# mLSTM and feed-forward on one core: other start addresses for the activation tiles and three of the output-weight tiles

## Chip, core and metric

One core of a Trainium2 chip runs the whole program. The metric is the device time of one execution in microseconds (us). The kernel before takes 466.67 us, the median of three runs (466.32 to 467.1).

## What is computed

A gated linear-attention recurrence (mLSTM) over 4 batches x 8 heads x 768 tokens with a head width of 40, and behind it a feed-forward of 3072 tokens x 320 channels through 2048 hidden channels:

```python
m_new  = max(f[t] + m, i[t])
f_stab = exp(f[t] + m - m_new);  i_stab = exp(i[t] - m_new)
C = f_stab * C + i_stab * outer(v[t], k[t])
n = f_stab * n + i_stab * k[t]
y[t] = sigmoid(o[t]) * (C @ q[t]) / max(abs(n . q[t]), 1)
...
h = x @ w_in                       # x: y of all heads side by side, 3072 x 320
out = (max(h, 0) + alpha * min(h, 0)) @ w_out
```

## The kernel before

The recurrence is computed in chunks of 128 tokens, two chunks make a group of 256 tokens, and there are twelve groups. Each group's attention result is transposed, so that channels lie on partitions, and split into a high and a low part (`x_tiles_of`, `split_steps`): XH and XL hold channels 0 to 255 (two slices of 256 tokens), X2 and X2L the last 64 channels. All matmuls of the feed-forward work on such float32r pairs.

**Up** (`FeedForward.up_steps`, lines 713 to 720). A step makes two of the 16 blocks of 128 hidden channels: for each, eight matmuls accumulate in PSUM. The stationary operand is a 128x128 piece of a weight tile (WH, WL or W2), the moving one a slice of 256 tokens of XH, XL, X2 or X2L. Eight steps a group and twelve groups make 96 steps, so 1536 matmuls of 256 columns.

**Down** (`FeedForward.down`, line 750). The hidden activations, again as a high part gh and a low part gl, are the stationary operand (128x128 pieces). The moving operand is a 320-column row of the output weights, of the high tile OH or the low tile OL. There are four OH tiles and four OL tiles (OH0 to OH3, OL0 to OL3), each with four rows. A step issues eight matmuls that alternate between OH and OL, each such pair with the same piece of gh, and then four of gl with OH. This makes 12 matmuls a step and, with 96 steps, 1152 in all.

```python
def high(e, j):
    add(e, j, gh, OH, start=fp + e == 0, stop=False)
    add(e, j, gh, OL, start=False, stop=False)
def low(e, j):
    add(e, j, gl, OH, start=False, stop=2 * fp + e == NF - 1)
```

In group 1 the first four steps keep gh and gl in one tile gg (tags sp0 and sp1) rather than in the tiles of the late pool.

**Order.** The order of all work is a list of step names (`ORDER` and `PATTERN`), and `pin` ties each engine to it. TensorE runs the steps of the feed-forward between the chunks' small matmuls; ScalarE, VectorE and GpSimd make g, gh and gl from the PSUM tile ph, and the SyncE queue issues the DMAs.

**Places.** A tile's start within a partition comes from the order in which the pools hand out room: the pool `const` holds the weights and the constants, behind it lie the pool `sb` (attention tiles, X's tiles) and the pool `late` (g, gh, gl, ob). While weights are loaded as 64-bit words, the places of OH1, OL1 and so on serve as staging tiles first (`staging`, with the table `ROOM`), so `staging` is what claims the place of OL1, OL2 and OL3. `LPs` holds two tiles of 512 bytes a partition for a three-part copy of the decay rows; the steps lqa to lqe that would fill the first of them (LP0) are defined but stand in no order list.

Of the kernel before, what the change touches and what calls it, by code (L numbers as in the profile page):

```python
# [8 lines left out]
F32 = mybir.dt.float32  # L9
F32R = mybir.dt.float32r  # L10
U32 = mybir.dt.uint32
BF16 = mybir.dt.bfloat16
# [5 lines left out]
def kernel(ctx: ExitStack, tc: tile.TileContext, q, k, v, i_gate, f_gate, o_gate, w_in, w_out, alpha, out):  # L18
# [3 lines left out]
    P = 128  # L22
    BH = B * H
# [3 lines left out]
    GT = GC * P  # L27
# [6 lines left out]
    const = ctx.enter_context(tc.tile_pool(name="const", bufs=1))  # L34
# [30 lines left out]
    def out_block(i):  # L65
        OH[i] = const.tile([P, NB, DM], F32R, tag=f"OH{i}", name=f"OH{i}")
        OL[i] = const.tile([P, NB, DM], F32R, tag=f"OL{i}", name=f"OL{i}")

    def staging(name, tag):
        t = const.tile([P, NB * DM], U32, tag=tag, name=name)  # L70
        return t[:, : 2 * CW].rearrange("p (c w) -> p c w", w=2)

# [10 lines left out]
    C_t = [const.tile([P, H, VA], F32, tag=f"C{i}", name=f"C{i}") for i in range(3)]  # L83
    L_d = dram.tile([NC, BH, P], F32, tag="L_d", name="L_d")

    LPs = [const.tile([3 * BH, GT], BF16, tag=f"LP{k}", name=f"LP{k}") for k in range(2)]
    unit = const.tile([BH, 1], F32, tag="unit", name="unit")
    gam = const.tile([BH, NC], F32, tag="gam", name="gam")
    const.tile([P, 64], F32, tag="room", name="room")
# [761 lines left out]
    def load_w_in(i, kt):  # L851

        c0 = i * CW
        half, h0 = divmod(c0, DH)

        def part(X):

            def at():
                if X[half] is None:
                    in_half(half)  # L860
                return X[half][:, kt, h0 : h0 + CW]

            return at

        src = w_in[kt * P : (kt + 1) * P, c0 : c0 + CW]
        return Weights(f"wi{i}_{kt}", staging(f"wi{i}_{kt}", ROOM[i][kt]), [(slice(0, P), src, part(WH), part(WL))])

    def load_w_rest(i):

        pieces = []  # L870
        for e in range(2):
            cs = slice((i + e) * CW, (i + e + 1) * CW)
            rows, other = (slice(x * KR, (x + 1) * KR) for x in (e, 1 - e))
            pieces.append((rows, w_in[2 * P :, cs], W2[rows, cs], W2[other, cs]))
        return Weights(f"wr{i}", staging(f"wr{i}", ROOM[i][2]), pieces)
# [44 lines left out]
    def first_group():  # L920
# [14 lines left out]
        f, i, rst, m = fi[:, 0, :S], fi[:, 1, :S], rm[:, 0, :S], rm[:, 1, : S + 1]  # L935
# [171 lines left out]
        def one(it):  # L1107
            return lambda: next(it)
# [3 lines left out]
        def add(names, it):  # L1112
            for name in names.split():
                steps[name] = one(it)
# [14 lines left out]
        def lazily(make):  # L1129

            def run():
                yield from make()
            return run()

        def alpha_by_token():
            pa = psa("pa")
            nc.tensor.transpose(pa[:, :NF], al, ident[:NF, :NF])
            yield
            nc.vector.tensor_scalar(oma, pa[:, :NF], -1.0, 1.0, ALU.mult, ALU.add)
            yield  # L1140
# [25 lines left out]
        def decay_parts(k, tag):  # L1166

            rest = late_pool.tile([P, 512], F32, tag=tag, name=f"L_rest{k}", bufs=3)[:BH]
            rest, mid = rest[:, :GT], rest[:, GT:].bitcast(BF16)[:, :GT]
            Lt, LP = L[:, k * GT : (k + 1) * GT], LPs[k]  # L1170
            nc.scalar.copy(LP[:BH], Lt)
            yield
            nc.gpsimd.tensor_tensor(rest, Lt, LP[:BH], ALU.subtract)
            yield
            nc.scalar.copy(mid, rest)
            yield
            nc.scalar.copy(LP[BH : 2 * BH], rest)
            yield
            nc.gpsimd.tensor_tensor(LP[2 * BH :], rest, mid, ALU.subtract)
            yield  # L1180
# [59 lines left out]
            do2=lambda: load_gate(0, nc.sync, 2 * GC, NC), do3=lambda: load_gate(1, nc.sync),  # L1240
        )
        add("lpa lpb lpc lpd lpe", lazily(lambda: decay_parts(1, "gl")))
        add("lqa lqb lqc lqd lqe", lazily(lambda: decay_parts(0, "gh")))
        add("alT alC", alpha_by_token())
        add("bTt bTc", by_token(bj, bT, "b", 0, 0, GC))
        add("wTt wTc", by_token(wj, wT, "w", 0, 0, GC))
# [61 lines left out]
    start = len(nc.cur_bb.bb.instructions)  # L1308
    ffs = {}
    first = first_group()  # L1310
    next(first)
    pin(start)
# [30 lines left out]
```

## Time and profile before

| | |
|---|---|
| median of three runs | 466.67 us (466.32 to 467.1) |
| the profiled execution's own time | 465.87 us |
| its span, first to last instruction | 464.2 us |
| TensorE busy | 458.3 us, 99% of the span |
| weight loads busy | 447.5 us |
| VectorE, ScalarE, GpSimd busy | 308.7, 313.8, 309.1 us |
| DMA engines, mean busy share | 58.1% by the main queue |
| granted TensorE clock | 1.000 |

TensorE's matmul time and its weight loads are two rows that overlap: a matmul's record reaches from the start of its stream to its last result, so records of neighbours overlap too, and what a matmul costs is read from the distance between two starts.

### The profile page before, as it was taken

How to read it: one execution, taken by the hardware profiler on the slowest of the kernel's cores; microseconds unless marked ns; L12 is line 12 of the kernel's file. 1: busy time of each engine (PE TensorE's matmuls, PEld its weight loads, DVE VectorE, ACT ScalarE, POOL GpSimd, SP SyncE). 2: the span in 40 equal slices, each digit the busy share in tenths (PEclk: the TensorE clock that was granted, in tenths of full speed). 3: DMA queues.
4: the chain of work that ended last, by engine and by line, in shares of the span. 5: the costliest groups of instructions: out<-in, count | busy, mean ns of one | idle time of the engine just before them, and what ended most of it. 6: DMA issues, size and time to landing. Idle time of an engine off the chain costs nothing.

```text
span 464.2 us, 11823 instructions
## 1 busy us (share of the span) xinstructions
PE 458.3 (99%) x4434; PEld 447.5 (96%) x4434; DVE 308.7 (67%) x659; ACT 313.8 (68%) x714; POOL 309.1 (67%) x398
## 2 busy tenths in 40 slices
PE   8999999999999999999999999999999999999997
PEld 6889999999999999999999999999999999999996
DVE  4798999576866766766666775775675675663321
ACT  4799998858857857758758758658758658423331
POOL 7635656746879579479779589479789587224241
PEclk9999999999999999999999999999999999999999
DMA  8998897759694573696783683598572341000000
GB/s 187 215 269 196 221 254 213 141 133 186 150 144 113 138 160 96 133 184 160 137 169 91 125 181 97 117 186 172 128 165 84 96 136 42 1 28 1 30 2 28
DMA packets 156163, 61.61 MB, mean 133 GB/s; under 512 B 140154, under 2 KB 145834, under 8 KB 156106
## 3 DMA queue, kind: packets, MB, share of 16 engines
q1 hardware_dynamic: 156026, 60.75, 58.1%
q8 instruction: 35, 0.57, 0.5%
q14 instruction: 22, 0.18, 0.1%
q10 hardware_dynamic: 80, 0.11, 0.1%
HBM read 36.90 MB, written 4.03 MB: 88 GB/s over the span
## 4 chain that ended last, share of the span: by engine, by line
PE 90%; DVE 4%; ACT 2%; SPq 2%; DMA 1%; issue 1%; DVEq 0%; ACTq 0%
PE po L750 36%; PE ph L713 5%; PE ph L718 5%; PE ph L716 5%; PE ph L714 5%; PE ph L717 5%; PE ph L720 5%; PE ph L715 5%; PE ph L719 5%; PE pH L376 4%; PE pS L477 4%; PE pH L337 1%; PE p L566 1%; PE pu L181 1%; PE pI L401 1%; PE pS L1071 1%
## 5 line engine op out<-in xcount | busy, mean ns | idle before, releaser
L739 POOL TENSOR_TENSOR gl<-g,gh 128x512 fp32r<-128x512 f32 x74 | 95.9, 1297 | 37.6 <-ACT gh L737 30.8
L750 PE MATMUL po<-OH,gh 128*128 128x320 f32 x368 | 110.4, 311 | 0.0
L750 PE MATMUL po<-OL,gh 128*128 128x320 f32 x368 | 109.3, 309 | 0.0
L723 ACT ACTIVATE g<-ph 128x512 f32<-128x512 f32 x96 | 57.4, 598 | 72.1 <-PE ph L720 66.5
L728 DVE SCALAR_TENSOR_TENSOR g<-g,oma,ph 128x256 f32<-128x256 f32 x148 | 63.5, 471 | 37.3 <-ACT g L723 37.3
L750 PEld LDWEIGHTS po<-OL,gh 128*128 128x128 f32 x368 | 69.2, 188 | 0.0
L750 PEld LDWEIGHTS po<-OH,gh 128*128 128x128 f32 x368 | 69.1, 188 | 0.0
L750 PE MATMUL po<-OH,gl 128*128 128x320 f32 x368 | 69.1, 309 | 0.0
L713 PE MATMUL ph<-XH,WH 128*128 128x256 f32 x192 | 57.6, 300 | 0.5 <-DVE g L728 0.5
L750 PEld LDWEIGHTS po<-OH,gl 128*128 128x128 f32 x368 | 57.7, 188 | 0.3 <-DVE gl L739 0.3
L718 PE MATMUL ph<-XL,WH 128*128 128x256 f32 x192 | 53.7, 280 | 0.0
L714 PE MATMUL ph<-XH,WH 128*128 128x256 f32 x192 | 53.6, 279 | 0.0
L716 PE MATMUL ph<-XH,WL 128*128 128x256 f32 x192 | 53.6, 279 | 0.0
L717 PE MATMUL ph<-X,W 128*128 128x256 f32 x192 | 53.6, 279 | 0.0
L719 PE MATMUL ph<-XL,WH 128*128 128x256 f32 x192 | 53.6, 279 | 0.0
L715 PE MATMUL ph<-XH,WL 128*128 128x256 f32 x192 | 53.6, 279 | 0.0
L720 PE MATMUL ph<-X2L,W 128*128 128x256 f32 x192 | 53.6, 279 | 0.0
L363 ACT CAST E<-pS 128x512 bf16<-128x512 f32 x72 | 41.1, 581 | 15.2 <-DVE pS L360 14.6
L448 ACT ACTIVATE E<-Lb,gates 128x128 f32<-128x128 f32 x160 | 50.1, 393 | 0.0
L737 ACT CAST gh<-g 128x512 fp32r<-128x512 f32 x74 | 44.7, 617 | 7.4 <-DVE g L728 4.9
L360 DVE TENSOR_TENSOR pS<-pS,E 128x512 f32<-128x512 f32 x36 | 24.9, 696 | 31.3 <-PE pS L477 23.5
L451 POOL TENSOR_SCALAR_AFFINE_SELECT E<-E 128x512 f32<-128x512 f32 x40 | 26.7, 668 | 20.4 <-ACT E L448 20.3
(196 smaller groups left out, 1136.8 us busy)
## 6 DMA issues: line engine op xcount, KB each, us to landing
Lb<-L_d SPq DMA_DIRECT2D x20, 512.0 KB
wo<-in_moe_w_out_dram SPq DMA_DIRECT2D x8, 640.0 KB
wi<-in_moe_w_in_dram SPq DMA_DIRECT2D x8, 512.0 KB
qn<-in_q_dram SPq DMA_DIRECT2D x24, 160.0 KB
kn<-in_k_dram SPq DMA_DIRECT2D x24, 160.0 KB
og<-in_o_gate_dram SPq DMA_DIRECT2D x24, 160.0 KB
va<-in_v_dram SPq DMA_DIRECT2D x24, 160.0 KB
out_dram<-ob SPq DMA_DIRECT2D x11, 320.0 KB
```

Of the source, the lines that this page charges most:

```text
L713: nc.tensor.matmul(dst, WH[half][:, 0, hs], XH[:, 0], start=True, stop=False)
L714: nc.tensor.matmul(dst, WH[half][:, 1, hs], XH[:, 1], start=False, stop=False)
L715: nc.tensor.matmul(dst, WL[half][:, 0, hs], XH[:, 0], start=False, stop=False)
L716: nc.tensor.matmul(dst, WL[half][:, 1, hs], XH[:, 1], start=False, stop=False)
L717: nc.tensor.matmul(dst, W2[:, fs], X2, start=False, stop=False)
L718: nc.tensor.matmul(dst, WH[half][:, 0, hs], XL[:, 0], start=False, stop=False)
L719: nc.tensor.matmul(dst, WH[half][:, 1, hs], XL[:, 1], start=False, stop=False)
L720: nc.tensor.matmul(dst, W2[:, fs], X2L, start=False, stop=True)
L723: nc.scalar.activation(gt, ph, AF.Relu, scale=-1.0)
L728: nc.vector.scalar_tensor_tensor(out=y[:, e], in0=gt[:, e], scalar=oma[:, f : f + 1], in1=ph[:, e], op0=ALU.mult, op1=ALU.add)
L739: (nc.vector if split else nc.gpsimd).tensor_tensor(gl, y, gh.bitcast(F32), ALU.subtract)
L750: nc.tensor.matmul(po[j], x[:, e, j * P : (j + 1) * P], W[f // NB][:, f % NB], **ends)
```

## The change

Three edits in the set-up code; all 8136 instructions of the built program, their order and their waits are the same in both kernels, and only the addresses differ.

```diff
+    GAP = {"OL1": 16, "OL3": 48, "OL2": 32}
+
     def staging(name, tag):
+        if tag in GAP:
+            const.tile([P, GAP.pop(tag)], F32, tag=f"gap{tag}", name=f"gap{tag}")
         t = const.tile([P, NB * DM], U32, tag=tag, name=name)
...
-    LPs = [const.tile([3 * BH, GT], BF16, tag=f"LP{k}", name=f"LP{k}") for k in range(2)]
+    LPs = [None, const.tile([3 * BH, GT], BF16, tag="LP1", name="LP1")]
...
-        add("lqa lqb lqc lqd lqe", lazily(lambda: decay_parts(0, "gh")))
```

Unused tiles of 64, 192 and 128 bytes are put ahead of OL1, OL3 and OL2, in the order in which those are claimed, and LP0 (512 bytes) goes. The places that the pools give, in bytes of a partition:

| tiles | start before | modulo 256 | start now | modulo 256 |
|---|---|---|---|---|
| W2 | 17408 | 0 | 17408 | 0 |
| WH1, WL1, WH0, WL0 | 47616 to 72704 | 0 | 512 less | 0 |
| OH0, OL0 | 80896, 86016 | 0, 0 | 512 less | 0, 0 |
| OH1, OL1 | 91136, 101376 | 0, 0 | 90624, 100928 | 0, 64 |
| OH2, OL2 | 96256, 116736 | 0, 0 | 95744, 116608 | 0, 128 |
| OH3, OL3 | 106496, 111616 | 0, 0 | 106048, 111360 | 64, 0 |
| Lb, kS, Z (gg), E, og, kd, qS | 121856 to 174080 | 0 | 128 less | 128 |
| XH, XL, X2, X2L | 188224 to 199488 | 64 | 128 less | 192 |
| gl, g, gh, ob | 208192 to 226624 | 64 | 128 less | 192 |

The tiles ahead of LP0 (qn, kn, va, gates, C and the smaller constants) stay where they were. The two va tiles start at 33792 and 36480, which is 0 and 128 modulo 256, and the second chunk in each lies 1344 bytes further on, at 64 and 192.

## Rows read from the trace of the kernel before

**Rows 1.** The page: busy time, TensorE's clock in 40 slices, chain by engine.

```profile
PE 458.3 (99%) x4434; PEld 447.5 (96%) x4434; DVE 308.7 (67%) x659; ACT 313.8 (68%) x714; POOL 309.1 (67%) x398
...
PEclk9999999999999999999999999999999999999999
...
PE 90%; DVE 4%; ACT 2%; SPq 2%; DMA 1%; issue 1%; DVEq 0%; ACTq 0%
```

**Rows 2.** The page's groups, down and up matmuls: out<-in, count, busy us, mean ns.

```profile
L750 PE MATMUL po<-OH,gh 128*128 128x320 f32 x368 | 110.4, 311 | 0.0
L750 PE MATMUL po<-OL,gh 128*128 128x320 f32 x368 | 109.3, 309 | 0.0
...
L750 PE MATMUL po<-OH,gl 128*128 128x320 f32 x368 | 69.1, 309 | 0.0
L713 PE MATMUL ph<-XH,WH 128*128 128x256 f32 x192 | 57.6, 300 | 0.5 <-DVE g L728 0.5
...
L714 PE MATMUL ph<-XH,WH 128*128 128x256 f32 x192 | 53.6, 279 | 0.0
```

**Rows 3.** Waits of TensorE: total us, times, longest us.

```profile
PE warm L154 <- POOL ident masks.py:199: 1.4, 1, 1.4
PE ph L713 <- DVE g L728: 0.5, 1, 0.5
PE pg L1161 <- DVE gates L979: 0.4, 1, 0.4
PE pb L1030 <- DVE E L1075: 0.3, 1, 0.3
```

**Rows 4.** The chain from 443 us on: start us, length us, what; repeats merged.

```profile
443.06 0.11 PE ph L714
...
444.88 0.11 PE ph L714
...
446.46 0.12 PE ph L720
446.58 1.76 PE po L750 x12
448.33 0.12 PE ph L713
...
450.22 0.12 PE ph L713
...
452.10 8.81 PE po L750 x60
```

**Rows 5.** All matmul records of line 714: duration ns min/median/max.

```profile
L714 PE MATMUL ph<-XH,WH x192: 276/280/283, 34.8 to 451.1; 128*128 128x256 f32 x192
```

**Rows 6.** The whole chain: a bfloat16 stretch of 256 columns, and a down stretch.

```profile
28.08 0.44 PE warm L154 x4
...
81.74 3.52 PE po L750 x24
```

**Rows 7.** Instructions that touch the tile gg: duration ns, first and last start.

```profile
L750 PE MATMUL po<-OH,gg x32: 308/309/389, 76.1 to 88.5; 128*128 128x320 f32 x32
```

**Rows 8.** GpSimd and ScalarE reading the two va tiles: duration ns min/median/max.

```profile
L349 POOL TENSOR_TENSOR vr<-va,vb x18: 819/828/1287, 78.2 to 380.6; 128x336 f32<-128x336 f32 x18
...
L347 ACT CAST vb<-va x18: 462/472/475, 77.5 to 374.4; 128x336 bf16<-128x336 f32 x18
```

**Rows 9.** Two stretches: busy us of each engine, clock, DMA share, GB/s.

```profile
0.00:60.00 60.00, 57.93 (x528) 51.81 (x529) 46.92 (x97) 48.93 (x111) 34.78 (x58) 1.00 0.91 221
60.00:464.20 404.20, 400.41 (x3908) 395.69 (x3906) 261.80 (x563) 264.89 (x605) 274.35 (x340) 1.00 0.54 120
```

## The prediction

> **What bounds the kernel now.** I read the page first. TensorE's matmul row is busy for 458.3 of 464.2 us, its clock is fully granted in all 40 slices, and the chain that ended last lies on TensorE for 90% [rows 1]. It waits for others hardly at all: its four waits sum to 2.6 us [rows 3]. So the time is the sum of the distances between matmul starts, and nearly all of it lies in two kinds of matmul, those of the up step (256 columns) and of the down step (320 columns) [rows 2].
>
> Records of neighbours overlap, so I take distances from starts in the chain. The last group shows both kinds with little else running [rows 4]. In the first up stretch, L714 at 443.06 and L714 sixteen matmuls on at 444.88 are 1.82 us apart: **113.8 ns** each. In the next one, L713 at 448.33 and L713 sixteen on at 450.22 are 1.89 us apart: **118.1 ns** each. The down stretch takes 8.81 us for 60, **146.8 ns** each. All of it runs at the full clock [rows 1].
>
> The reader should see two things here. First, both are longer than the columns need: four bfloat16 matmuls of 256 columns in a row take 0.44 us, 110 ns each [rows 6]. By that, 320 columns would take 137.5 ns. The surplus is 8.1 ns on an ordinary up matmul and 9.3 ns on a down matmul. Second, the same up step on the same tiles exists in two states, 4.35 ns apart. Which is common can be read from the length of the records of L714: shortest 276, median 280, longest 283 ns [rows 5], and their mean is 279 [rows 2]. If 276 is the short state and 280 the ordinary one, at most a quarter are short. I take 1,400 of 1,536 up matmuls as ordinary.
>
> **The change part by part.** It adds, removes and moves no instruction. No wait is added and no queue changes, so each edit can act only through what one instruction takes at its new addresses.
>
> *LP0 and the steps lqa to lqe go.* No instruction ever used them: 0 us.
>
> *VectorE, ScalarE and GpSimd at other addresses.* GpSimd reads the va tiles at all four places modulo 256 that occur here (0, 64, 128 and 192) in 819 ns at the least and 828 ns in the median; ScalarE does in 462 to 475 ns [rows 8]. An effect of the place is under 3% of such an instruction. These engines are busy for 65 to 68% of the time outside the first 60 us [rows 9], and TensorE waits for VectorE 0.5 us once in that path [rows 3]. 0 us, and 3% more on each would still be hidden.
>
> *DMAs to and from other places.* Most staging tiles and the attention tiles now start off the 256-byte mark. In the first 60 us the DMA engines are busy for 0.91 of the time, after that for 0.54 [rows 9]. Transfers that take a tenth longer would still fit into the idle 5.4 us of the first stretch, DMA has 1% of the chain [rows 1], and TensorE waits for none [rows 3]: 0 us. Without that cover, a tenth of 60 us would be late at most.
>
> *Stationary gh at 192 instead of 64, against OH at 0.* The tile gg gives this for another place: it starts at 0 modulo 256, and all down matmuls between 76.1 and 88.5 us use it [rows 7]. The stretch of 24 at 81.74 lies inside and takes 3.52 us, 146.7 ns each [rows 6], against 146.8 with gh at 64 [rows 4]. Moving the stationary operand 64 bytes against the moving one did nothing. I take 0 for this edit. No row has a difference of 128 or 192. The bounds are therefore the whole surplus as a gain, 1,152 x 9.3 ns = 10.7 us, and as a loss the largest step between two states that the rows hold, the 4.35 ns of the up step: 1,152 x 4.35 ns = 5.0 us. I keep to 0, since the one shift that the trace holds gave 0.
>
> *OL1, OL2, OL3 and OH3 off the 256-byte mark.* Before, each stream of a down step starts at the place where the one before it ended, because 1,280 bytes are five times 256. Now the pairs OH1-OL1, OH2-OL2 and OH3-OL3 jump by 64, 128 and 192 bytes there and back. A jump occurs in the trace only where an up stretch (X at 64) meets a down stretch (OH at 0). There the last up matmul to the first down matmul is at 446.46 to 446.58, 0.12 us by the rounding of the chain, so a jump costs or saves less than what a row shows. I take 0, with the same bounds as above for three quarters of the down matmuls.
>
> *X's tiles at 192 instead of 64, against W at 0.* This is the term that I expect to move. The two states of the up step show that 4.35 ns hang on how its two operand streams meet, since the tiles, the clock and the shapes are the same in both. The start of the moving stream against the weights is what the change shifts, by half of the 256 bytes. If every ordinary stretch went to the short state, that would be 1,400 x 4.35 ns = 6.1 us; if none did, 0; if all went as far the other way, 6.1 us more. Both states recur in the trace with one and the same pair of addresses, so the place does not fix the state alone. I take half of the stretches: 700 x 4.35 ns = **3.0 us gained**. TensorE ahead by 3 us in 464 asks 0.7% more of the other engines, which their idle third covers.
>
> The profiled execution would go from 465.87 us (span 464.2 and 1.7 around it) to 462.9. It lies 0.8 below the median of 466.67, so the median goes to **463.7 us**.
>
> At one place a rule speaks against any effect at all. The Trainium skill, "TensorE: Matmul & The Clock Gate", section "Step-by-step: what each phase is for", says that TensorE has two independent read ports, one for the streaming operand and one for the weight load, so that loading the next weights takes nothing from the running matmul. By that rule no place could matter and the sum would be 0. The equal down stretches [rows 4, 6] agree with it; the two states of the up stretch [rows 4] do not obviously, since something other than columns and clock sets them.
>
> **The rivals.**
>
> *No effect.* The surplus is a fixed cost of 4-byte operands, and the state of an up stretch comes from when it starts and not from where its tiles lie. For it: gg against gh, and two states with the same addresses [rows 4, 6, 7]. Against it: sums of over 2,600 matmuls have to agree to 0.35 ns each to stay within 0.93 us. Time 466.7. Chance 0.25.
>
> *The short state is lost, or a third, longer one appears.* Place: the up stretches and the down matmuls with OL1 to OL3, where streams now start away from where the last one ended. Price: as far above the ordinary distance as the short one is below, 4.35 ns. It decides from 214 matmuls on (0.93 us), 14 of the 96 up steps or a fifth of the down ones. For half of the up matmuls and none of the down ones it gives 3.0 us, 469.7 us; for all up ones 472.8. For it: before the change the stationary operand of the down step starts 64 bytes behind the moving one modulo 256 (gh at 64, OH at 0), and that step carries the larger surplus; after it the up step has this difference (W at 0, X at 192). Against it: the short state is rare already, so little can be lost there. Chance 0.30.
>
> That the change does not do what it says is excluded: the addresses are those of the built program.
>
> **How the numbers follow.** Faster by the up stretches, or by the down ones, has chance 0.45 and, at half of the ordinary up stretches, 463.7 us. About 0.2%, 0.93 us, is what a measurement of this kernel can tell from no change; the first rival has all of the middle, 0.25, and the second is all of the slower side, 0.30. The range: its low end is all up stretches short (6.1 us) and a third of the down bound (3.5 us), 457 us; its high end takes the second rival to nearly all up stretches, 472 us. The likeliest case alone reaches from 457 to 465.7.
>
> **What would show it.** Right: two L714 starts sixteen matmuls apart in the middle groups stand 1.82 us apart and not 1.89, and the median record of L714 falls from 280 towards 276 ns, while a down stretch stays near 146.7 ns a matmul. Down stretches that take less than 146 ns or more than 148 ns on OL1, OL2 or OL3 but not on OL0 would show that I sized the jumps wrong at 0. DMAs are the cause if starts at 60 us are later and the distances are the same. The forecast is wrong if the up stretches keep 118.1 ns everywhere, and its sign is wrong if they take 120 ns or more.

## The result and the profile after

The changed kernel takes **462.08 us** (median of four runs, 461.66 to 462.53) against 466.5 us of the kernel before beside it (465.71 to 467.1): ratio 0.9907, 95% interval 0.9888 to 0.9925. That is 4.4 us less by the medians. The profiled execution has an own time of 461.96 us and a span of 460.2 us, 4.0 us less than the 464.2 of before.

The page after, to be laid beside [rows 1]: busy time, TensorE's clock, the chain by engine.

```profile
PE 454.4 (99%) x4434; PEld 443.7 (96%) x4434; DVE 310.1 (67%) x659; ACT 314.0 (68%) x714; POOL 308.5 (67%) x398
...
PEclk9999999999999999999999999999999999999999
...
PE 90%; DVE 4%; ACT 2%; SPq 2%; DMA 1%; issue 1%; DVEq 0%; ACTq 0%
```

TensorE's busy time fell by 3.9 us, nearly all of the span's 4.0; no other engine moved by more than 1.4 us, the clock is full in all 40 slices in both, and the chain has the same shares. So the time went out of the matmuls themselves, at the same clock. The groups of matmuls and TensorE's waits after, to be laid beside [rows 2] and [rows 3]:

```profile
L754 PE MATMUL po<-OH,gh 128*128 128x320 f32 x368 | 109.8, 311 | 0.0
L754 PE MATMUL po<-OL,gh 128*128 128x320 f32 x368 | 108.9, 307 | 0.0
...
L717 PE MATMUL ph<-XH,WH 128*128 128x256 f32 x192 | 57.5, 299 | 0.4 <-DVE g L732 0.4
```

```profile
PE warm L158 <- POOL ident masks.py:199: 1.4, 1, 1.4
PE ph L717 <- DVE g L732: 0.4, 1, 0.4
PE pg L1165 <- DVE gates L983: 0.3, 1, 0.3
PE pb L1034 <- DVE E L1079: 0.3, 1, 0.3
```

The groups' means hardly move, since records overlap. The distances show it. The chain over the last two up stretches after, for [rows 4]: start us, length us, what.

```profile
439.15 0.12 PE ph L717
...
441.10 0.11 PE ph L718
...
442.80 1.74 PE po L754 x12
444.54 0.12 PE ph L717
...
446.38 0.11 PE ph L717
...
448.20 8.79 PE po L754 x60
```

Each up stretch here has 32 matmuls. The last one lasts from 444.54 to 448.20: 3.66 us, 114.4 ns each, where before it lasted from 448.33 to 452.10: 3.77 us, 117.8 ns each [rows 4]. Within it the first sixteen take 1.84 us (115 ns each) and the second sixteen 1.82 us (113.8 ns each): the stretch begins long and goes over to the short state. The down stretch of 60 takes 8.79 us against 8.81 [rows 4]. The records of one line, for [rows 5]:

```profile
L718 PE MATMUL ph<-XH,WH x192: 276/277/287, 34.8 to 447.2; 128*128 128x256 f32 x192
```

The median fell from 280 to 277 with the shortest still 276: the short state was there before, and now most matmuls are in it. The two stretches of the span, for [rows 9]:

```profile
0.00:60.00 60.00, 57.95 (x531) 51.91 (x531) 47.41 (x97) 49.10 (x111) 34.20 (x58) 1.00 0.91 221
60.00:460.20 400.20, 396.46 (x3907) 391.77 (x3904) 262.64 (x563) 264.95 (x604) 274.30 (x340) 1.00 0.55 121
```

By 60 us TensorE has run 531 matmuls against 528 before, with the same DMA share of 0.91, so the transfers to the new places do not show as a delay. The 4.0 us come from the 400 us behind.

To see the whole, I summed the distance from each matmul record's start to the next one's over the trace of each run, apart for the 1,536 up matmuls, the down matmuls and the rest (small matmuls and every wait between). From before to after the up sum goes from 184.53 to 181.14 us (3.39 less), the down sum from 170.11 to 169.63 (0.48 less), the rest from 104.53 to 104.45. Those add to 3.94 us, the 4.0 of the span. Up matmuls at 115 ns or less (the short state, mean 113.4 ns) went from 175 to 1,012, those between 115 and 125 ns from 1,312 (mean 117.8 ns) to 474 (mean 118.5). Some 50 are left in each; 43 of these are the first matmul of a stretch, which takes some 200 ns both before and after. Of the 79 unbroken up stretches, 5 before and 66 after are short: their mean distance from the ninth matmul on is at most 115 ns. The table of the experiments holds these sums for all runs.

### The profile page after: what moved, and what is told of

Its sections match the earlier page's. It is cut to its first block, busy times and chain, and to the rows that moved or that the text cites. A ratio compares the mean times of both kernels' runs of the same rounds, so it can differ in the third digit from the quotient of the medians.

```text
span 460.2 us, 11823 instructions
## 1 busy us (share of the span) xinstructions
PE 454.4 (99%) x4434; PEld 443.7 (96%) x4434; DVE 310.1 (67%) x659; ACT 314.0 (68%) x714; POOL 308.5 (67%) x398
## 4 chain that ended last, share of the span: by engine, by line
PE 90%; DVE 4%; ACT 2%; SPq 2%; DMA 1%; issue 1%; DVEq 0%; ACTq 0%
PE po L754 36%; PE ph L717 5%; PE ph L720 5%; PE ph L718 5%; PE ph L719 5%; PE ph L722 5%; PE ph L721 5%; PE ph L724 5%; PE ph L723 5%; PE pH L380 4%; PE pS L481 4%; PE pH L341 2%; PE p L570 1%; PE pu L185 1%; PE pI L405 1%; PE pS L1075 1%
```

## The experiments

The theory to be tested: what counts is where X's tiles start against the weights modulo 256 bytes, and the other edits do little. Against it: the gain comes from the jumps of the OL tiles, from gh and the other late tiles, from LP0, or from the absolute place of X. The sums of all runs:

| run | up us | down us | rest us | matmuls up to 115 ns | short stretches of 79 | median us, ratio to before [95%] |
|---|---|---|---|---|---|---|
| before | 184.53 | 170.11 | 104.53 | 175 | 5 | 466.5 |
| after | 181.14 | 169.63 | 104.45 | 1,012 | 66 | 462.08, 0.9907 [0.9888, 0.9925] |
| e1_x_alone | 181.53 | 169.91 | 104.72 | 874 | 49 | 462.94, 0.9930 [0.9914, 0.9947] |
| e2_ol_alone | 184.17 | 169.71 | 105.35 | 265 | 12 | 465.38, 0.9981 [0.9967, 0.9994] |
| e3_lp0_out | 184.85 | 170.10 | 104.98 | 112 | 4 | 466.57, 1.0013 [1.0002, 1.0023] |
| e4_late_alone | 185.13 | 170.03 | 105.50 | 17 | 1 | 466.23, 1.0005 [0.9994, 1.0017] |
| e5_w_moved | 180.90 | 170.30 | 105.29 | 1,051 | 60 | 462.9, 0.9920 [0.9905, 0.9935] |
| e6_x_at_0 | 187.79 | 170.16 | 106.33 | 9 | 0 | 468.99, 1.0061 [1.0038, 1.0084] |
| e7_x_at_128 | 186.46 | 169.92 | 104.95 | 292 | 0 | 467.7, 1.0024 [1.0013, 1.0035] |
| e8_all_64 | 181.27 | 169.24 | 105.55 | 959 | 64 | 462.01, 0.9899 [0.9882, 0.9915] |
| e9_x_at_224 | 185.94 | 170.15 | 105.50 | 69 | 0 | 467.42, 1.0021 [1.0011, 1.0031] |
| e10_x_at_160 | 185.56 | 169.98 | 105.15 | 171 | 0 | 467.19, 1.0014 [1.0000, 1.0027] |
| e11_ol_192 | 180.73 | 169.68 | 105.01 | 1,088 | 69 | 462.46, 0.9910 [0.9894, 0.9925] |
| e12_x_at_96 | 188.16 | 170.07 | 105.34 | 67 | 0 | 469.27, 1.0065 [1.0053, 1.0078] |

The rest varies between 104.5 and 106.3 us from profile to profile (in e6, which has the most, the granted clock was 0.86 between 12 and 24 us, before the first up matmul), so a difference of under 1 us is read from the up and down sums and from the times together, not from one span.

### One part at a time

**X alone at 192** (e1). LP0 is out as in the change; padding keeps everything but X's tiles where it was modulo 256.

```diff
     def x_tiles_of(g):
+        if g == 0:
+            sb.tile([P, 32], F32, tag="xpad", name="xpad", bufs=1)
...
     late_pool = ctx.enter_context(tc.tile_pool(name="late", bufs=2))
+    late_pool.tile([P, 32], F32, tag="lpad", name="lpad", bufs=1)
```

> LP0 is out, and of all tiles only X's start at another place modulo 256: 192 instead of 64. gh, gl, the attention tiles and the OL tiles keep their places modulo 256 (everything behind LP0 lies 512 bytes lower). Theory X (the place of X against the weights sets the state of the up stretches): up stretches lock at 113.3 ns a matmul as in the changed kernel, the sum of the up distances falls from 184.5 to about 181.1 us, the time by 3 to 4 us to about 463. Theory OL (the jumps of the down step hand the up stretches another start, and that sets their state): no change, 466.5 us, up at 117.8 ns. Theory late (the place of gh and the other late tiles): no change, 466.5 us.

Measured: 462.94 us against 466.24 beside it, 3.3 us less, with the up sum 3.0 us down. The last up stretch and the records of the line:

```profile
445.48 0.12 PE ph L715
...
449.11 8.80 PE po L752 x60
```

```profile
L716 PE MATMUL ph<-XH,WH x192: 276/278/282, 35.1 to 448.1; 128*128 128x256 f32 x192
```

3.63 us for 32 matmuls, 113.4 ns each. By the medians X alone brings three quarters of the change's 4.4 us; the intervals of the two ratios overlap.

**The jumps of OL1 to OL3 alone** (e2), with LP0 out and X back at 64.

```diff
+    GAP = {'OL1': 16, 'OL3': 48, 'OL2': 32}
...
+        if tag in GAP:
+            const.tile([P, GAP.pop(tag)], F32, tag=f"gap{tag}", name=f"gap{tag}")
...
+    sb.tile([P, 32], F32, tag="spad", name="spad", bufs=1)
```

> The gaps ahead of OL1, OL2 and OL3 as in the change, and all tiles behind them back at their old places modulo 512 (X and gh at 64). Theory X: up stretches stay at 117.8 ns, only the down step moves, by half a microsecond or less: 466 us. Theory OL: up stretches lock at 113.3 ns, about 463 us. Theory late: 466 us.

Measured: ratio 0.9981, about 0.9 us less. The chain over the last up stretch and the down stretch behind it:

```profile
448.44 0.12 PE ph L718
...
452.21 8.78 PE po L755 x60
```

The up stretch keeps its 3.77 us; the down stretch of 60 takes 8.78 us against 8.81. The down sum fell by 0.40 us, more than it differs between the other runs with X at 64 and no jumps (170.03 to 170.30). The up sum fell by 0.36 us, less than it differs between before, e3 and e4 (184.53 to 185.13), which have X at this place too. In this one profile the rest is 0.8 us longer and the span is the 464.2 us of before, so the 0.9 us stand on the ten executions and not on the profile. The jumps are not quite free of effect, then: they give a little in the down matmuls.

**LP0 out alone** (e3) and **the late pool alone at 192** (e4, gh, gl, g and ob, with X at 64). e3 has only the change's two lines on LP0; e4 has these and the line of the late pool from e1.

> Only LP0 and its unused steps are out: every tile behind it lies 512 bytes lower, W2 and the tiles ahead of it do not move. All three theories (X, OL, late): 466.5 us, no change, up at 117.8 ns and down at 146.7 ns. If it is faster by 3 us, the 512 bytes between W2 and the other weights, or the bits above 256, are the cause, and none of the three.

> LP0 is out, and the late pool alone (t, g, gl, gh, ob) starts at 192 instead of 64 modulo 256; X stays at 64, OL at 0. Theory X: up stretches stay at 117.8 ns, 466.5 us; the down step has its stationary operand moved by 128 against OH, which I forecast at 0. Theory late: up stretches lock at 113.3 ns or the down step falls below 146 ns a matmul, 463 us. Theory OL: no change.

Measured: 1.0013 and 1.0005, down sums 170.10 and 170.03 against 170.11. Both stay within 0.2% of before. The end of the chain in e4:

```profile
453.60 8.81 PE po L750 x60
```

The down stretch of 60 takes the 8.81 us of [rows 4], though gh now stands at 192 against OH at 0: moving the stationary operand of the down step did not move its time at this difference either, as gg had shown at another. The runs with X at 64 also say how firm the ordinary state is there: 112 short matmuls in e3, 17 in e4 and 265 in e2, against 175 before.

### The place of X against the place of W

**W moved instead of X** (e5): all up weights go to 128 modulo 256, X stays at 64, so the difference X minus W is 192 again, with neither at the place that it has in the change.

```diff
+    const.tile([P, 32], F32, tag="wpad0", name="wpad0")
     W2 = const.tile([P, DFF], F32R, tag="W2", name="W2")
+    const.tile([P, 32], F32, tag="wpad1", name="wpad1")
...
+        const.tile([P, 32], F32, tag="wpad2", name="wpad2")
         fi, rm = (const.tile([P, 2, DH], F32, tag=t, name=f"g_{t}") for t in ("WH1", "WL1"))
...
         in_half(0)
+        const.tile([P, 32], F32, tag="wpad3", name="wpad3")
         out_block(0)
```

> LP0 is out; all weights of the up step (W2, WH, WL) start at 128 instead of 0 modulo 256, and X stays at 64: the difference of X minus W modulo 256 is 192, as with X alone moved, but reached from the other side. All other tiles keep their places modulo 256. Theory relative (only the difference between X and the weights counts): up stretches lock at 113.3 ns, up sum about 181.5 us, time 463. Theory absolute (the place of the moving stream alone counts, or of X's writers): up stays at 117.8 ns, 184.8 us, time 466.5.

Measured: 0.9920, up sum 180.90, 60 short stretches. The last one:

```profile
445.79 0.12 PE ph L715
...
449.43 8.81 PE po L752 x60
```

3.64 us for 32, as in e1. It is the difference of the two operands' starts that counts, not the place of X by itself. The places also bear out the modulus for this difference: it is 192 modulo 512 in the change, 448 modulo 512 in e1, e8 and e11, and the short state is common in all four.

**X at 0, 128, 224, 160 and 96** (e6, e7, e9, e10, e12): e1 with other sizes of the two pads, so that only X's place differs from e3. The cut shows what e6 changes in e1.

```diff
-            sb.tile([P, 32], F32, tag="xpad", name="xpad", bufs=1)
+            sb.tile([P, 48], F32, tag="xpad", name="xpad", bufs=1)
...
-    late_pool.tile([P, 32], F32, tag="lpad", name="lpad", bufs=1)
+    late_pool.tile([P, 16], F32, tag="lpad", name="lpad", bufs=1)
```

> LP0 is out; X alone starts at 0 modulo 256 (difference to W: 0), everything else as with X alone at 192. Theory four places (the start of X against W in steps of 64 sets the state): some value of its own, between 113.3 and 120 ns on the up step, up sum between 180.5 and 187 us. Theory two places (192 is good, all others are alike): up at 117.8 ns, 184.8 us, 466.5.

> LP0 is out; X alone starts at 128 modulo 256 (difference to W: 128). Theory four places: a value of its own between 113.3 and 120 ns, up sum between 180.5 and 187 us. Theory two places: up at 117.8 ns, 184.8 us, 466.5.

> LP0 is out; X alone starts at 224 modulo 256, 32 bytes beyond 192, W at 0. Theory steps of 64 (what counts is which 64-byte piece of 256 both streams stand in): as X alone at 192, up sum about 181.5 us, time 463. Theory sliding (the distance itself counts, and 192 lies on a slope that leads to 0, where 120 ns was measured): up sum between 181.5 and 187.8 us, about 184.5, time 466.

> LP0 is out; X alone starts at 160 modulo 256, halfway between 128 (up sum 186.5 us) and 192 (181.5 us). Theory steps of 64: 160 stands in the same piece as 128, up sum about 186.5 us, time 467.7. Theory sliding: up sum about 184 us, time 465.5, or below 181.5 if the best place lies between.

> The kernel before without LP0, with X's tiles at 96 modulo 256 (W at 0, everything else as before modulo 256). So far only a difference of 192 gave many up matmuls of 113.3 ns; 0, 128, 160 and 224 gave 118 to 120 ns. 'One place': 192 stands alone, so 96 gives an up sum of 184.5 to 187 us, fewer than 300 matmuls of at most 115 ns, and 466.4 to 468 us. 'A second place': the good places recur within the 256 bytes (192 is good and 96 is half of it), so 96 gives an up sum near 181.5 us, over 800 such matmuls and 462.9 us.

Measured: all five are slower than before or at its edge, by 0.14% to 0.65%; e3, their control with X at 64, is 0.13% slower, so e7, e9 and e10 stand out from it by their up sums (185.56 to 186.46 against 184.85 us) and not by their times. The last up stretch of 32 in e6, e12 and e10, each with the first down row behind it:

```profile
453.38 0.12 PE ph L715
...
457.21 8.81 PE po L752 x60
```

```profile
452.68 0.12 PE ph L715
...
456.52 8.81 PE po L752 x60
```

```profile
449.87 0.12 PE ph L715
...
453.63 8.81 PE po L752 x60
```

At a difference of 0 the stretch takes 3.83 us, 119.7 ns each; at 96 3.84 us, 120.0 ns; at 160 3.76 us, 117.5 ns. In the other two it takes 3.80 us at 128 (118.8 ns) and 3.79 at 224 (118.4 ns). The down stretch of 60 is the same 8.81 us in all three rows, so the down step did not move. The median over the 79 stretches of their mean distances (from the ninth matmul on) is 120.0 at 0, 117.8 at 64, 120.0 at 96, 118.6 at 128, 117.6 at 160, **113.4 at 192**, 118.6 at 224. Thus there are more kinds of state than two. At 0 nearly every distance is 120 ns; the matmul records of e6, shown here, have a median of 283 ns where the ordinary state has 280, and the weight loads beside them, the first row, one of 192 ns where that line has 188 both before and after. At 96, 128, 160 and 224 a stretch has no steady distance: the last one of e12 repeats 117, 125, 116, 123, 119 and 120 ns. So the values of these four places are averages, and the 292 matmuls up to 115 ns of e7 are single ones within longer stretches.

```profile
L716 PEld LDWEIGHTS ph<-XH,WH x192: 187/192/192, 36.6 to 456.1; 128*128 128x128 f32 x192
L716 PE MATMUL ph<-XH,WH x192: 278/283/296, 36.7 to 456.2; 128*128 128x256 f32 x192
```

The place is neither a slope (160 and 224, the neighbours of 192 at 32 bytes, have no short stretch at all) nor a pattern that repeats within 256 (96 is on average as slow as 0, where I had allowed up to 187 us for its up sum and it took 188.16). 192 stands alone among the seven places that were run. 32 was not run. All tiles of this program start at multiples of 32 bytes, so padding reaches no place between.

### The down step's pairs

**All four pairs 64 apart** (e8): the change, with each OL at 64 and each OH at 0. **OL at 192** (e11): the change, with OL1 to OL3 at 192, all else of the output weights at 0.

```diff
-    GAP = {"OL1": 16, "OL3": 48, "OL2": 32}
+    GAP = {'OH1': 48, 'OL1': 16, 'OH3': 48, 'OL3': 16}
...
+        if i == 0:
+            const.tile([P, 16], F32, tag="gapOL0", name="gapOL0")
```

```diff
-    GAP = {"OL1": 16, "OL3": 48, "OL2": 32}
+    GAP = {'OL1': 48, 'OH3': 16, 'OL3': 48}
```

In both, one more pad in the pool `sb` keeps the tiles behind at their places of the change modulo 256. The question is whether the distance within a pair sets the time of the down step, or something else.

> X, the attention tiles and the late tiles as in the change (192, 128, 192); all four OH tiles at 0 modulo 256 and all four OL tiles at 64. In the changed kernel the matmuls with OH1 and OL1 (0 and 64) took 437.2 ns for three against 440 ns before, those with OH2 and OL2 (0 and 128) 440.1. Theory pairs (the distance of OL from OH sets the down step, and 64 is worth 2.7 ns in three): the down sum falls by another 0.5 us to about 169.1 us, time about 461.5. Theory phase (what the down step gains depends on the order of states and not on the pair): down within 0.3 us of the changed kernel, 462.

> X, the attention tiles and the late tiles as in the change; OH tiles and OL0 at 0 modulo 256, OL1, OL2 and OL3 at 192. Theory pairs (the distance of OL from OH sets the down step): in the changed kernel OL3, 192 beyond its OH3, took 143.9 ns; with three such pairs the down sum falls by about 0.5 us against the changed kernel, to 169.1 us, time 461.5. Theory phase (the order of states decides): down within 0.3 us of the changed kernel's 169.6 us, time 462.

Measured: e8 462.01 us, e11 462.46 us, neither distinguishable from the 462.08 of the change. The end of the chain in e8, and in e11:

```profile
445.27 0.13 PE ph L720
...
449.05 8.77 PE po L757 x60
```

```profile
444.70 0.12 PE ph L718
...
448.35 8.82 PE po L755 x60
```

The down stretch of 60 holds steps of the pairs 1 to 3 (OH1 with OL1 and so on). It takes 8.77 us with the pairs 64 apart and 8.82 with them 192 apart. The down sums are 169.24 and 169.68: e8 came out near the 169.1 that the theory of pairs asked for, e11 at the 169.6 of the change that the theory of phase asked for.

The single tiles say more. In the change, where each pair has another distance, the mean distance from a matmul on OH or OL to the next one (without the few over 160 ns) was 146.1 and 147.1 ns in pair 0 (apart by 0), 144.9 and 146.6 in pair 1 (by 64), 148.0 and 144.6 in pair 2 (by 128), 146.8 and 143.9 in pair 3 (OH at 64, OL at 0), against 146.6 to 147.0 for all eight before. So a jump shifts time between the two matmuls of a pair and saves at most some 3 ns on one of them. In e11 the three pairs that are 192 apart differ among themselves: one matmul on OH, one on OL and one of gl together take 437.1 ns in pair 1 and 436.6 in pair 3, where OH has the saving (144.1 and 144.0 ns), but 441.3 in pair 2, where OL takes 149.2; before they took 439.9, 439.5 and 440.4. The distance within the pair modulo 256 alone does not set it, therefore. Modulo 512 pairs 1 and 3 of e11 are 192 apart and pair 2 is 448 apart; whether that is the reason, no run shows.

The e8 rows also hold a counter-example to a simple rule. X is at 192 there, and still the last up stretch takes 3.78 us for 32, 118.1 ns a matmul, and never reaches the short state. 15 of the 79 stretches of e8 stay out of the short state, and 13 of those of the change.

## Why the prediction was right

The forecast was 463.7 us, faster by the up stretches; measured were 462.08 us. For the profiled execution it was 462.9 against 461.96; of these 0.9 us, 0.4 are X's term, 0.5 the down step and 0.1 the rest. By its own steps:

- **What bounds the kernel.** Right. TensorE's busy time and the span fell by nearly the same amount (3.9 and 4.0 us), and no other engine followed or hindered it.
- **X at 192: half of 1,400 ordinary matmuls times 4.35 ns, 3.0 us.** Right in kind: one part alone (e1) does it, it depends on the difference between the operands' starts (e5), and it works by moving stretches into the short state that the trace before already held. The term was undersized: 3.4 us in the change's up sum. The price of a matmul was near (117.8 less 113.4 is 4.4 ns, 4.35 forecast). The share was not: I took half of the stretches, and 61 more of 79 went over. Against that stand fewer ordinary matmuls to begin with, 1,312 and not 1,400, and the stretches' first matmuls. 837 more short matmuls at 4.4 ns would be 3.7 us; 3.4 was left, since the 474 that stayed out take 118.5 ns on average and not 117.8 (0.3 us). Part of these stand at the start of a stretch, which begins long. The timeline of TensorE in the changed kernel shows such a beginning (start us, length us, engine, line, what):

```profile
439.10 0.28 PE L718 MATMUL ph<-XH,WH 128*128 128x256 f32 x1
...
439.58 0.28 PE L722 MATMUL ph<-XL,WH 128*128 128x256 f32 x1
439.69 0.28 PE L723 MATMUL ph<-XL,WH 128*128 128x256 f32 x1
...
440.03 0.28 PE L718 MATMUL ph<-XH,WH 128*128 128x256 f32 x1
440.14 0.28 PE L719 MATMUL ph<-XH,WL 128*128 128x256 f32 x1
```

From 439.10 to 439.58 it is four distances of 120 ns each; from 439.69 to 440.14 four of 112.5, both within the rounding of the rows. This stretch goes over after some six matmuls. In most stretches of the change four or five distances are long first, in most of e1 and e5 two.
- **Why half.** The reason given, that the place does not fix the state alone, holds: in e8 one stretch with X at 192 is ordinary throughout. But "shifted by half of the 256 bytes" was not what made the difference: moving X by that half from 0 to 128 gains 1.3 us in the up sum and leads to no short stretch. The trace before had rows of one difference alone, 64, so it could show that a short state exists, not at which difference it is common. The sign was therefore a choice between two sides, as the chance of 0.45 said, and that it came out faster was luck: of the six other places that were run against 64, only 192 is faster.
- **gh at 192: 0.** Right, by e4 (170.03 against 170.11 us).
- **LP0, the other engines, the DMAs: 0 each.** Right for LP0, by e3 (within 0.2%). For the others the rows after agree: TensorE's waits sum to 2.4 us against 2.6, and the two stretches show no delay. The attention tiles at 128 were not run alone.
- **The jumps of OL1 to OL3: 0.** Mis-sized, slightly. The change's down sum fell by 0.48 us and e2's by 0.40 (e1's, without any jump, by 0.20); e2's time says 0.9 us, with an interval from 0.3 to 1.5. The sign that the prediction named for this came: under 146 ns on OL2 and OL3 (144.6 and 143.9), not on OL0 (147.1). The argument for 0, one jump at the seam of two stretches that cost less than a row shows, could not see 3 ns on a matmul of 147.
- **Rival "No effect".** Fallen, since e1 and e5 exclude it. The rule of the Trainium skill that was held against the change ("TensorE: Matmul & The Clock Gate", section "Step-by-step: what each phase is for", two independent read ports) gave 0 for every place as the prediction read it, and the runs do not agree with that reading: 113.4 against 120.0 ns at the full clock, for one and the same instructions, by the place alone. Whether the weight load takes anything from the running matmul is a narrower question that these runs do not answer. The down step's indifference to gh agrees with the rule.
- **Rival "the short state is lost, or a third, longer one appears".** The third state exists, and at half its price: 120.0 ns, 2.2 above the ordinary one where 4.35 were assumed. It belongs to the difference 0 and, as an average, to 96, not to 192. The evidence that it gave, the down step's surplus at "stationary 64 behind moving", was no guide to the up step. Had X been moved by 64 the other way, to 0, this rival would have been the outcome: e6, 468.99 us.

What sets these states is not shown by any run. That the weight load's stream and the moving stream of the matmul beside it meet in some way that depends on their starts modulo 256 is an argument from the trace (both run at the same time, 443.7 and 454.4 us of 460.2, and in e6 the weight load's records lengthen too, from 188 to 192 ns), and no experiment here took the one away from the other. Why X alone leaves 30 stretches out of the short state, e5 19, and the change, e8 and e11 only 10 to 15, is open too. Each count is from one execution, and the medians of e1 and e5 (462.94 and 462.9 us) do not differ. The late tiles with X at 192 and everything else as before were not tried.

## What to carry to other kernels

Where TensorE bounds a kernel, measure the distance between starts of equal matmuls in several stretches: two values at one clock and one shape are a reason to try whether the operands' placement has a price, which here was up to 6.6 ns of 120 on each. Then try the place of the moving tile against the stationary one in steps of 32 bytes over 256, one pad at a time, since here the neighbours of the good place gave no hint of it. Keep padding that decides such a thing in named tiles, because removing an unused tile ahead of it shifts everything behind. Taking out LP0 alone, 512 bytes or twice 256, changed the time by no more than 0.2%.

## What was not expected of the hardware

For float32r matmuls of 256 columns the distance between starts at the full clock was 113.4 ns at one place of seven (192 bytes modulo 256 from weights to moving tile) and 117.6 to 120.0 on average at the others, where four bfloat16 matmuls in a row take 110 ns each [rows 6]. A stretch finds its state on the way: in the change mostly after four or five long distances, in e1 and e5 after two. For 320 columns the places that were run moved a matmul by some 3 ns at the most.
